# Second mixture: hand-written order in the first three quads, a plain last product, block sums placed anew

## The chip, the cores and the metric

The kernel runs on one core of one Trainium2 chip. The metric is the device time of one execution in microseconds. The core has TensorE (PE in the profile, its weight loads PEld), VectorE (DVE), ScalarE (ACT), GpSimd (POOL) and SyncE (SP), whose queue issues nearly all DMAs here.

## The reference

Attention with a feature map gives x (2304 rows of 512). A first mixture sends each row to one of 8 experts. The part that the change touches is the second mixture: every row goes through all 8 experts, weighted by a matrix P that is normalized eight times by rows and columns.

```python
def _moe2_ref(x, w_gate, w1, w2):          # N, D, E, F = 2304, 512, 8, 1024
    logits = x @ w_gate
    P = np.exp(logits - logits.max())
    for _ in range(8):
        P /= P.sum(1, keepdims=True) + 1e-09
        P /= P.sum(0, keepdims=True) + 1e-09
        P *= N / E
    out = np.zeros((N, D), dtype=np.float32)
    for e in range(E):
        h = np.maximum(x @ w1[e], 0.0)
        out += P[:, e:e + 1] * (h @ w2[e])
    return out
```

## The kernel before

The second mixture is `moe2`. Every float32 operand is split into a rounded high part (ACT, the `..._high` functions) and the rest (DVE, `..._low`), and a product takes three matmuls: high by high, high by low, low by high.

The rows are worked on in three passes of 768 rows (two halves of 3 tiles of 128). A pass runs over 16 weight sets (8 experts, two quarters of the hidden width each). One pass over one weight set is a quad; there are 48 (`NQD`), 16 in a pass (`NW`), and the second pass takes the sets in reverse, so that set 0 is used by quads 31 and 32 in a row. The first product of a quad (x by w1) is done by a scheme of seven block products instead of eight (`mm`, banks `pa`, `pb`, `pd`): numbers 1, 6, 7, 2, 5, 3, 4 in this order, each of six matmuls of 384 columns for each of two halves g of the hidden block. A quad (n) has two groups (n, 0) and (n, 1).

In the first pass the second product is plain: a `piece` is one tile of 128 rows by 512 columns in 12 matmuls. `group` writes out the order of one group: products, copies, splits, and three places `fill[0..2]` for the three pieces of the quad before. `high[k]` and `low[k]` are the splits that ride along: of w2 in group (n, 0), of the next w1 in group (n, 1). Sums of weight blocks (`sums_w2`, `sums_w1`, on POOL) feed further splits, which are stored to HBM (`wd1`, `wd2`) for the later passes: `sums_low` issues two stores right after its split, `store_w2` three, `store_w1` one of 512 KB for each of four operands.

Quads 0 to 2 (`AUTO`) are left to the compiler's scheduler, which orders them freely. They also hold work that occurs once: the rows of the other two passes are loaded, transposed, multiplied by the gate weights and stored (`other_logits`), and P is normalized (`sinkhorn_start`, `sinkhorn_step`). From quad 3 on everything stands in `manual_schedule`: each queue, SP's too, follows the order of the program. After quad 2 the sums of quads 0 and 1 are scaled by P and P is stored (lines 1319 to 1321).

In passes two and three both products use the seven-block scheme. `first` issues the products of the first layer, `h_of` applies the rectifier and P, POOL combines the hidden blocks (tile `R`), `high` and `low` split them into `H` (groups A to D). `unit` is one product of the second layer, six matmuls into a bank of its own (14 per quad, for the quad before), and `flush` adds it to one of seven block accumulators M1 to M7 in `Z`, on DVE, or by a copy on ACT and a sum on POOL for the five k in `GFL`. At the end of a pass the seven blocks are combined and the four result blocks are transposed and written out (`out_tile`, or `turn_part` and `send` for the last pass). The order is written as a list of times in slots, `at(time, function)`, sorted at the end; 14 slots are a quad, and the times only give the order.

## Time and profile before

| | us |
|---|---|
| median of 3 runs | 1955.12 (1946.89 to 1956.08) |
| profiled execution | 1944.32 |
| its span, first to last instruction | 1942.6 |
| first pass, groups (0,0) to (3,0) | 137.16 (429.40 to 566.56) |
| a steady group of the first pass | 15.6 |
| turn from pass two to pass three | about 1458 to 1478 |
| end, from the last first-layer product | 1908.4 to 1942.6 |

A group is taken from the start of its first copy of bank `pa` (`s<-pa`, line 1126) to that of the next group. In a timeline row stand the start in us from the span's start, the time in us, the engine, the line, the operation, the tiles written and read and the count; in brackets the engine's idle time before it and what ended it. PEclk is the granted share of TensorE's clock.

### The profile page before, as it was taken

The page shows a single profiled execution, that of the slowest core. Times are in us where ns is not written, and L with a number is a line of the kernel's source. Part 1 is how long each engine was busy: PE and PEld are TensorE (multiplying, and loading weights), DVE is VectorE, ACT ScalarE, POOL GpSimd, SP SyncE. Part 2 cuts the span into 40 slices and gives each one's busy share as a digit, 9 for nine tenths or more (in the row PEclk, how much of TensorE's full clock was granted, in tenths as well). Part 3 has the DMA queues.
Part 4 walks back from the last instruction along what each step waited for, and adds up shares of the span by engine and source line. Part 5 has one row for each costly group of instructions (what it writes and reads, how often), then busy time and mean ns, then how long its engine had stood idle before and what let it go on. Part 6 is the DMA issues. An engine that isn't in the chain of part 4 may idle for free.

```text
span 1942.6 us, 34972 instructions
## 1 busy us (share of the span) xinstructions
PE 1892.5 (97%) x13028; PEld 1781.2 (92%) x13028; DVE 1347.6 (69%) x2309; ACT 931.5 (48%) x1679; POOL 747.1 (38%) x652
## 2 busy tenths in 40 slices
PE   9999899989999999999999999999999999999997
PEld 8998799966789988888899999999999999999997
DVE  5777777764876776767757667667786676676665
ACT  5776555545544544444444444444444444444442
POOL 2011442211424343434125445444663444444445
PEclk9999999999999999999999999999999999999999
DMA  7324696648757777777476776777756767767663
GB/s 187 100 65 113 163 332 219 212 145 266 261 201 246 260 244 263 253 256 275 161 241 218 231 238 219 237 240 248 238 170 227 240 219 235 233 219 250 224 202 109
DMA packets 232532, 420.67 MB, mean 217 GB/s; under 512 B 31567, under 2 KB 149215, under 8 KB 232349
## 3 DMA queue, kind: packets, MB, share of 16 engines
q1 hardware_dynamic: 228732, 410.93, 64.5%
q0 software_dynamic: 3456, 7.30, 1.0%
q8 instruction: 106, 1.74, 0.4%
q14 instruction: 78, 0.63, 0.1%
q10 hardware_dynamic: 160, 0.07, 0.0%
HBM read 311.18 MB, written 109.50 MB: 217 GB/s over the span
## 4 chain that ended last, share of the span: by engine, by line
PE 68%; DVE 3%; POOL 1%; DMA 1%; issue 1%; ACT 1%; SPq 0%; POOLq 0%; DVEq 0%; ACTq 0%
PE pu L1357 23%; PE pb L1118 14%; PE py L1153 12%; PE pd L1118 9%; PE pa L1118 9%; POOL acc L1447 1%; POOL hr L1447 0%; DVE hh L1404 0%; DMA acc<-in_moe_w_dram 0%; DVE hh L1139 0%; DVE wc L882 0%; DVE xcl L1016 0%; DMA w<-wd 0%; DVE acc L1372 0%; DVE hr L1396 0%
## 5 line engine op out<-in xcount | busy, mean ns | idle before, releaser
L1357 PE MATMUL pu<-hh,w 128*128 128x384 f32 x2688 | 540.4, 336 | 8.0 <-DVE acc L1447 4.2
L1357 PEld LDWEIGHTS pu<-hh,w 128*128 128x128 f32 x2688 | 473.4, 188 | 9.5 <-DVE acc L1447 4.6
L1447 POOL TENSOR_TENSOR hr<-hr 128x384 f32<-128x384 f32 (+1 forms) x192 | 282.3, 1470 | 289.2 <-DVE hr L1396 166.5
L1118 PE MATMUL pb<-xch,wc 128*128 128x384 f32 x1152 | 297.8, 339 | 1.7 <-ACT v L1126 0.6
L1400 ACT ACTIVATE hh<-hr 128x384 fp32r<-128x384 f32 (+2 forms) x256 | 189.3, 761 | 207.5 <-POOL hr L1447 155.2
L1153 PE MATMUL py<-w,hh 128*128 128x512 f32 x1152 | 287.5, 396 | 0.0
L1404 DVE TENSOR_TENSOR hh<-hr,hh 128x384 fp32r<-128x384 f32 (+2 forms) x256 | 223.1, 881 | 62.8 <-ACT hh L1400 61.5
L1153 PEld LDWEIGHTS py<-w,hh 128*128 128x128 f32 x1152 | 215.4, 189 | 43.1 <-issue 1.9
L1370 POOL TENSOR_TENSOR acc<-acc,s 128x384 f32<-128x384 f32 x147 | 161.9, 1102 | 223.9 <-ACT s L1369 223.8
L1372 DVE TENSOR_TENSOR acc<-pu,acc 128x384 f32<-128x384 f32 x267 | 147.3, 553 | 103.9 <-PE pu L1357 103.0
L1118 PEld LDWEIGHTS pb<-xch,wc 128*128 128x128 f32 x1152 | 210.1, 188 | 9.6 <-ACT v L1126 1.5
L1118 PE MATMUL pa<-xch,wc 128*128 128x384 f32 x768 | 198.8, 338 | 0.1
L1118 PE MATMUL pd<-xch,wc 128*128 128x384 f32 x768 | 197.4, 338 | 0.3 <-DVE c L1211 0.2
L1369 ACT ACTIVATE s<-pu 128x384 f32<-128x384 f32 x147 | 72.1, 491 | 162.0 <-PE pu L1357 161.9
L1118 PE MATMUL pb<-xcl,wc 128*128 128x384 f32 x576 | 148.8, 339 | 0.0
L1118 PEld LDWEIGHTS pa<-xch,wc 128*128 128x128 f32 x768 | 139.8, 187 | 4.0 <-ACT acc L1100 0.6
L1118 PEld LDWEIGHTS pd<-xch,wc 128*128 128x128 f32 x768 | 139.5, 187 | 1.2 <-DVE c L1211 0.9
L882 DVE TENSOR_TENSOR wc<-r,wc 128x512 fp32r<-128x512 f32 x170 | 130.6, 769 | 4.1 <-ACT wc L879 3.7
L879 ACT ACTIVATE wc<-r 128x512 fp32r<-128x512 f32 x170 | 105.8, 623 | 10.6 <-PE pa L1118 9.0
L1118 PEld LDWEIGHTS pb<-xcl,wc 128*128 128x128 f32 x576 | 105.0, 188 | 0.0
L1118 PE MATMUL pa<-xcl,wc 128*128 128x384 f32 x384 | 99.1, 338 | 0.0
L1118 PE MATMUL pd<-xcl,wc 128*128 128x384 f32 x384 | 98.8, 338 | 0.0
(270 smaller groups left out, 2990.2 us busy)
## 6 DMA issues: line engine op xcount, KB each, us to landing
w<-wd SPq DMA_DIRECT2D x224, 512.0 KB
wc<-wd SPq DMA_DIRECT2D x120, 512.0 KB
r<-in_moe_w_dram SPq DMA_DIRECT2D x108, 512.0 KB
wd<-wc SPq DMA_DIRECT2D x64, 512.0 KB
wd<-acc SPq DMA_DIRECT2D x128, 256.0 KB
wd<-w SPq DMA_DIRECT2D x96, 256.0 KB
r<-in_moe_w_dram SPq DMA_DIRECT2D x90, 256.0 KB
acc<-in_moe_w_dram SPq DMA_DIRECT2D x64, 256.0 KB
```

The costliest lines, as they stand in the source:

```text
L879: nc.scalar.activation(wc[i][:, 0], wsrc[i], AF.Copy)
L882: nc.vector.tensor_tensor(wc[i][:, 1], wsrc[i], f32(wc[i][:, 0]), ALU.subtract)
L1118: nc.tensor.matmul(dst, wc[i][:, w, kb, sl], xcb[i][x][:, kb], start=(start and m == 0), stop=(stop and m == 5), skip_group_check=True,)
L1153: nc.tensor.matmul(py, ht[:, i * P : i * P + P], w[:, wt], start=(m == 0), stop=(m == 11))
L1357: nc.tensor.matmul(pu, w[:, wl, kb, g2 * P : g2 * P + P], H[:, hx[kb][xl].start + o], start=(m == 0), stop=(m == 5))
L1369: nc.scalar.activation(tmp, pu, AF.Copy)
L1370: nc.gpsimd.tensor_tensor(t, t, tmp, ALU.add)
L1372: nc.vector.tensor_tensor(t, pu, t, ALU.add)
L1400: nc.scalar.activation(H[:, hx[g][0]], R[:, u:v], AF.Copy)
L1404: nc.vector.tensor_tensor(H[:, hx[g][1]], R[:, u:v], f32(H[:, hx[g][0]]), ALU.subtract)
L1447: eng.tensor_tensor(out_, a, b, op)
```

## The change

All 16 quads of the first pass now stand in the hand-written order. The work that occurs once is cut into small steps and put by `CHORES` behind named places of the groups of quads 0 to 2: `l0` to `l6` are the `low` places, `f0` to `f2` the `fill` places. `T(o, i)` transposes tile i of half-pass o, `L` multiplies it by the gate weights, `Q` turns the result; the row and column steps of the normalization are `rw` and `cl`. The stores of a quad's split weights are issued one group or one quad later than before. Set 0 of `wd1` is not stored any more; its operands are computed again for quads 31 and 32, and in two quads ahead of that `GFL` isn't used. At the turn the output tiles come 1.5 slots later. In the last quad the hidden blocks aren't combined; the second product is eight plain block products (`last_unit`) that add up in eight banks, with one more stored operand (`wd2[8]`), and the seven accumulators are combined on POOL ahead of them.

```diff
--- before.py
+++ after.py
-            r, dh, fh = {1: (a11, 0, 0), 2: (a12, 1, 0), 4: (a22, 1, 1)}[i]
+            r, dh, fh = {1: (a11, 0, 0), 2: (a12, 1, 0), 4: (a22, 1, 1), 7: (a21, 0, 1)}[i]
...
+        def gate_tile(o):
+            return acc0(4 + o % 2)[0:E, 0:TW]
+        def logits(o, src):
-            gt = big.tile([E, TW], F32, name="gt", tag="v")
-            nc.scalar.activation(gt, pg, AF.Copy)
+            nc.scalar.activation(gate_tile(o), pg, AF.Copy)
+        def turn_logits(o):
...
+        others = {}
+        def load_other(k):
+            if k < 12:
+                o, i = divmod(k, TB)
+                others[k] = load_x(tiles(1 + o // 2, o % 2)[i], Z[:, 3072 + D * (k % 2) : 3072 + D * (k % 2) + D])
+        def turn_other(o, i):
+            if i == 0:
...
+            k = TB * (o - 2) + i
+            sl = slice(i * P, i * P + P)
+            transposed(
+                others[k], lambda pt: [(x[:, :, sl], pt[:, 2 * b : 2 * b + 2]) for b, x in enumerate(others["x", o])]
+            )
+            load_other(k + 2)
+            if i == TB - 1:
+                dst = xtd[o // 2 - 1][o % 2].rearrange("(b p) t -> p b t", p=P)
+                for b, x in enumerate(others["x", o]):
+                    nc.sync.dma_start(dst[:, 2 * b : 2 * b + 2], x)
+        def other_logits(o):
+            logits(o, lambda kb: others["x", o][kb // 2][:, kb % 2])
...
-        def sinkhorn_start():
+        sk = {}
...
+        def sinkhorn_columns():
+            v = nc.vector
             pc = ps.tile([P, E], F32, name="pc", tag="T", bufs=2)
-            nc.tensor.matmul(pc, c["ones_f"], cs, start=True, stop=True)
+            nc.tensor.matmul(pc, c["ones_f"], sk["cs"], start=True, stop=True)
             cr = big.tile([P, 1, E], F32, name="cr", tag="cr")
             v.tensor_scalar(cr, pc.unsqueeze(1), 1e-9, None, ALU.add)
             v.reciprocal(cr, cr)
             v.tensor_scalar(cr, cr, float(NTOK // E), None, ALU.mult)
             v.tensor_tensor(lg, lg, cr.to_broadcast([P, NT, E]), ALU.mult)
+        def scale_accs(h):
+            for t in tiles(0, h):
+                nc.scalar.activation(accs[t], accs[t], AF.Copy, scale=lg[:, t, 0:1])
+        def turn_gates():
+            lt = sk["lt"] = Z[:, 5120 : 5120 + E * NT].rearrange("p (e t) -> p e t", e=E)
+            nc.vector.tensor_copy(lt, lg.rearrange("p t e -> p e t"))
...
+            if m == NW - 1:
+                nc.sync.dma_start(wd2[8][0][:, :, g], f32(t[:, :, QF:D]))
...
-        for i in (6, 7, 5, 3):
-            store_w1(0, i)
+        for k in range(2):
+            load_other(k)
...
+        T = lambda o, i: lambda: turn_other(o, i)
+        L = lambda o: lambda: other_logits(o)
+        Q = lambda o: lambda: turn_logits(o)
+        rw, cl = sinkhorn_rows, sinkhorn_columns
+        CHORES = {
+            (0, 0): [("l0", Q(0)), ("l1", Q(1), T(2, 0)), ("l3", T(2, 1)), ("f0", T(2, 2)), ("f1", L(2)),
+                     ("l5", T(3, 0)), ("l6", Q(2)), ("f2", T(3, 1), T(3, 2))],
+            (0, 1): [("l0", L(3)), ("l1", T(4, 0)), ("l2", Q(3)), ("l3", T(4, 1)), ("f0", T(4, 2)), ("f1", L(4)),
+                     ("l5", T(5, 0)), ("l6", Q(4)), ("f2", T(5, 1), T(5, 2))],
+            (1, 0): [("l0", L(5)), ("l2", Q(5)), ("l3", sinkhorn_a), ("f0", sinkhorn_b), ("f1", sinkhorn_c), ("f2", rw)],
+            (1, 1): [("l1", cl, rw), ("f0", cl, rw), ("f1", cl, rw), ("f2", cl, rw)],
+            (2, 0): [("f0", cl, rw), ("f1", cl, rw), ("f2", cl, rw)],
+            (2, 1): [("f0", cl), ("f1", lambda: scale_accs(0), turn_gates), ("f2", lambda: scale_accs(1), store_gates)],
...
-                if n == 0:
-                    fill = [lambda i=i: other_logits(*others[2 * g + i]) if i < 2 else None for i in range(3)]
-                else:
-                    fill = [lambda i=i: piece(n - 1, g, i) for i in range(TB)]
+                fill = [lambda i=i: piece(n - 1, g, i) for i in range(TB)] if n else [none] * 3
...
-                    low[3] = both(low[3], lambda: store_w2(n, 0))
+                    if n == NW - 1:
+                        low[3] = both(low[3], lambda: store_w2(n, 0))
+                    if n:
+                        low[2] = both(low[2], lambda: store_w2(n - 1, 0))
+                        for k, i in zip((0, 1, 3, 4), (6, 7, 5, 3)):
+                            low[k] = both(low[k], lambda i=i: store_w1(n, i))
                     low[6] = both(low[6], lambda: sums_w2(n))
...
-                        def lo(i=i):
-                            w1_low(i, n + 1)
-                            if i in (6, 7, 5, 3):
-                                store_w1(n + 1, i)
-                        low[k] = lo
+                        low[k] = lambda i=i: w1_low(i, n + 1)
...
-                if g:
+                if g and n == NW - 1:
                     low[0] = both(low[0], lambda: store_w2(n, 1))
+                if g and n:
+                    low[1] = both(low[1], lambda: store_w2(n - 1, 1))
                 lead = [lambda: x_logits(0), lambda: x_logits(1)] if n == 0 and g == 0 else ()
+                for place, *fs in CHORES.get((n, g), ()):
+                    lst = fill if place[0] == "f" else low
+                    k = int(place[1])
+                    lst[k] = both(lst[k], *fs)
...
-                if n == 0 and g:
-                    sinkhorn_start()
-                if 1 <= n <= 2:
-                    sinkhorn_step()
-                    sinkhorn_step()
-        for n in range(AUTO):
-            quad(n)
-        for t in accs:
-            nc.scalar.activation(accs[t], accs[t], AF.Copy, scale=lg[:, t, 0:1])
-        store_gates()
...
+        part = lambda hx, o: {g: [slice(r.start + o, r.start + o + 1) for r in hx[g]] for g in range(2)}
+        raws.update({"E": (part(HC, 0), 1, 2), "F": (part(HD, 1), 4, 5)})
...
+            if NW + i == NQD - 1:
+                op = (1, 8, 2, 4)[j]
+                nc.sync.dma_start(f32(op_tile(s)), wd2[op][0 if op == 8 else key(wid[NW + i])])
+            else:
+                nc.sync.dma_start(f32(op_tile(s)), wd2[SORD[j]][key(wid[NW + i])])
...
-            elif k in GFL:
+            elif k in GFL and key(wid[min(NW + i + 2, NQD - 1)]):
...
-            for n in range(AUTO, NW):
+            for n in range(NW):
...
+                    if n == NQD - 1:
+                        at(t + 6.52, c21, g)
+                        at(t + 7.0, lambda n=n: h_of(n, 0, 4, st["c"]))
+                        e = 8.05 if g == 0 else 6.45
+                        at(t + e, high, "E", g)
+                        at(t + e + 0.35, low, "E", g)
+                        e = 12.05 if g == 0 else 7.1
+                        at(t + e, high, "F", g)
+                        at(t + e + 0.35, low, "F", g)
+                        continue
...
+                    if key(m) == 0:
+                        at(B0 - 7, load_raw, m, 7)
+                        g = nc.gpsimd
+                        at(B0 + 4.6, tt, g, s1, a21, a22)
+                        at(B0 + 4.7, tt, g, s2, s1, a11, ALU.subtract)
+                        at(B0 + 4.8, tt, g, a21, a11, a21, ALU.subtract)
+                        at(B0 + 10.4, tt, g, a12, a12, s2, ALU.subtract)
+                        for op, e in ((6, 7.6), (7, 8.6), (5, 10.6), (3, 12.6)):
+                            at(B0 + e, w1_high, op)
+                            at(B0 + e + 0.5, w1_low, op)
...
-                at(B0 + 12.3 + k, out_tile, 1, 1 - k // TB, k % TB)
+                at(B0 + 13.8 + k, out_tile, 1, 1 - k // TB, k % TB)
...
-            i = NQD - NW - 1
-            for s in range(14):
-                at(B0 + s + 0.5, unit, i, s)
-            for s in range(8):
-                at(B0 + s + 1.02, flush, i, s)
-            at(B0 + 2.1, tt, G, M2, M2, M1)
-            at(B0 + 2.2, tt, G, M6, M6, M1)
-            at(B0 + 6.1, tt, G, M3, M3, M5)
-            at(B0 + 6.2, tt, G, M3, M3, M6)
-            at(B0 + 8.1, tt, V, M7, M7, M6)
-            at(B0 + 8.2, tt, V, M5, M5, M7)
-            at(B0 + 8.3, tt, G, M4, M4, M7)
-            for g2 in range(2):
...
+            for e, X, Y in (
+                (6.2, M3, M5), (10.2, M6, M1), (12.1, M2, M1), (12.2, M7, M6), (12.3, M3, M6), (12.4, M5, M7), (14.1, M4, M7)
+            ):
+                at(B0 - 14 + e, tt, G, X, X, Y)
             fin = {}
+            banks = [("C12", 0, "pb"), ("C11", 1, "pb"), ("C12", 1, "Y"), ("C21", 0, "Y"), ("C22", 0, "T"),
+                     ("C21", 1, "T"), ("C22", 1, "pd"), ("C11", 0, "pa")]
+            nb = {"pa": 1, "pb": 2, "pd": 1, "Y": 2, "T": 2}
+            def fin_banks():
+                for nm, g2, tag in banks:
+                    fin[nm, g2] = ps.tile([P, TW], F32, name="pf", tag=tag, bufs=nb[tag])
+            def last_unit(nm, j, B, g2, start):
+                w = op_tile(7 * (NQD - NW - 1) + j)
+                m = 0
+                for wl, xl in ((0, 0), (0, 1), (1, 0)):
+                    for kb in range(2):
+                        hx = {"B11": HA, "B22": HB, "B12": raws["E"][0], "B21": raws["F"][0]}[B]
+                        nc.tensor.matmul(
+                            fin[nm, g2], w[:, wl, kb, g2 * P : g2 * P + P], H[:, hx[kb][xl].start],
+                            start=(start and m == 0), stop=(not start and m == 5), skip_group_check=True,
+                        )
+                        m += 1
+            def last_sum(X, nm, g2):
+                tt(V, X[:, g2], fin[nm, g2], X[:, g2])
...
+            at(B0 + 0.45, fin_banks)
+            u = 0
+            for nm, j, B, start, X in (
+                ("C11", 0, "B11", True, None), ("C21", 1, "B11", True, None), ("C12", 2, "B22", True, None),
+                ("C22", 3, "B22", True, None), ("C12", 0, "B12", False, M3), ("C22", 1, "B12", False, M5),
+                ("C11", 2, "B21", False, M2), ("C21", 3, "B21", False, M4),
+            ):
+                for g2 in range(2):
+                    at(B0 + 0.5 + u, last_unit, nm, j, B, g2, start)
+                    if X is not None:
+                        at(B0 + 1.1 + u, last_sum, X, nm, g2)
+                    u += 1
+            for dh in range(2):
+                for g2 in range(2):
+                    for k in range(TB):
+                        at(B0 + 13.7, turn_part, 1, k, dh, g2)
+            for k in range(TB):
+                at(B0 + 13.8, send, 1, k)
+            for dh in range(2):
+                for g2 in range(2):
+                    for k in range(TB):
+                        at(B0 + 17, turn_part, 0, k, dh, g2)
+            for k in range(TB):
+                at(B0 + 18, send, 0, k)
```

## Rows read from the trace of the kernel before

**Rows 1.** The page: busy time by engine, and the clock in 40 slices

```profile
PE 1892.5 (97%) x13028; PEld 1781.2 (92%) x13028; DVE 1347.6 (69%) x2309; ACT 931.5 (48%) x1679; POOL 747.1 (38%) x652
...
PEclk9999999999999999999999999999999999999999
```

**Rows 2.** Timeline of TensorE at the end: start us, us, engine line op

```profile
1908.38 7.47 PE L1357 MATMUL pu<-hh,w 128*128 128x384 f32 x42
1918.39 6.54 PE L1357 MATMUL pu<-hh,w 128*128 128x384 f32 x36 [2.54 <-DVE acc L1372]
1929.18 4.21 PE L1357 MATMUL pu<-hh,w 128*128 128x384 f32 x12 [4.25 <-DVE acc L1447]
1933.18 3.58 PE L1556 MATMUL pt<-ident,acc 128*128 128x128 f32 x24
```

**Rows 3.** Windows: us, then busy time of each engine; PEclk, DMA share, GB/s

```profile
429.40:566.56 137.16, 127.40 (x610) 97.79 (x609) 97.27 (x204) 69.89 (x135) 43.09 (x43) 0.98 0.69 231
...
544.39:566.56 22.17, 19.56 (x84) 16.36 (x83) 15.37 (x28) 10.29 (x19) 7.49 (x7) 0.85 0.44 147
707.91:723.54 15.63, 15.63 (x80) 14.14 (x79) 10.67 (x16) 6.63 (x13) 7.50 (x7) 1.00 0.67 220
723.54:739.14 15.60, 15.60 (x80) 14.10 (x79) 11.78 (x20) 8.19 (x16) 4.38 (x7) 1.00 0.80 288
```

**Rows 4.** Timeline of all engines at the turn to the third pass

```profile
1461.57 0.41 PE L1431 MATMUL pt<-ident,acc 128*128 128x128 f32 x2 [2.20 <-DVE acc L1447]
1462.22 0.54 DVE L1413 TENSOR_TENSOR z<-pd,z 128x384 f32<-128x384 f32 x1
...
1462.35 0.44 PE L1431 MATMUL pt<-ident,acc 128*128 128x128 f32 x2 [0.37 <-DVE acc L1447]
...
1476.73 1.32 PE L1357 MATMUL pu<-hh,w 128*128 128x384 f32 x6 [0.90 <-ACT xq L1433]
```

**Rows 5.** Timeline of POOL at the end

```profile
1921.58 6.96 POOL L1447 TENSOR_TENSOR acc<-acc 128x768 f32<-128x768 f32 x3
```

**Rows 6.** Windows of the end, as in group 3

```profile
1918.00:1932.00 14.00, 9.36 (x45) 9.04 (x46) 8.24 (x15) 0.00 (x0) 10.38 (x6) 0.86 0.01 1
1932.00:1943.00 11.00, 4.77 (x29) 4.43 (x27) 2.00 (x4) 2.28 (x4) 0.00 (x0) 0.81 0.38 143
```

**Rows 7.** Timeline of all engines in the first quad

```profile
429.27 2.75 PE L949 MATMUL pg<-xq,wg 128*8 128x384 f32 x8
...
440.65 1.11 SPq L934 DMA_DIRECT2D acc<-x2d  x2
...
441.66 0.68 DVE L1104 TENSOR_TENSOR acc<-acc 128x512 fp32r<-128x512 f32 x1
...
442.42 1.19 SPq L1106 DMA_DIRECT2D wd<-acc  x2
...
443.52 0.63 PE L941 MATMUL pt<-ident,acc 128*128 128x128 f32 x4 [0.17 <-DMA acc<-x2d]
```

**Rows 8.** Timeline of ACT at the end

```profile
1938.78 0.60 ACT L1560 ACTIVATE xq<-pt 128x512 f32<-128x512 f32 x1 [1.59 <-DVE xq L1561]
```

**Rows 9.** Timeline of DVE: one step of the normalization in the third quad

```profile
543.79 0.16 DVE L1048 TENSOR_SCALAR cr<-pc 128x8 f32<-128x8 f32 x1
...
545.32 0.27 DVE L1041 RECIPROCAL rs<-rs 128x18 f32<-128x18 f32 x1
...
546.86 0.43 DVE L1044 TENSOR_REDUCE cs<-lg 128x8 f32<-128x144 f32 x1
```

**Rows 10.** One line of the kernel: durations in ns, min/median/max

```profile
L1042 DVE TENSOR_TENSOR lg<-lg,rs x8: 287/301/1043, 497.6 to 546.0; 128x144 f32<-128x144 f32 x8
```

**Rows 11.** Timeline of all engines in a steady quad

```profile
708.39 1.18 SPq L857 DMA_DIRECT2D r<-in_moe_w_dram  x2
...
727.65 0.62 ACT L1100 ACTIVATE acc<-acc 128x512 fp32r<-128x512 f32 x1
...
730.60 0.49 ACT L1126 ACTIVATE z<-pb 128x384 f32<-128x384 f32 x1 [1.80 <-PE pb L1118]
```

More of the change, by code (lines that the diff above doesn't have):

```diff
@@ L943, in transposed @@
                 copy(d, s)
-        def logits(ps_, h, src):
+        def gate_tile(o):
+            return acc0(4 + o % 2)[0:E, 0:TW]
+        def logits(o, src):
             pg = ps.tile([E, TW], F32, name="pg", tag="T", bufs=2)
@@ L949, in logits @@
                 nc.tensor.matmul(pg, wg[:, kb], src(kb), start=(kb == 0), stop=(kb == NKB - 1))
-            gt = big.tile([E, TW], F32, name="gt", tag="v")
-            nc.scalar.activation(gt, pg, AF.Copy)
+            nc.scalar.activation(gate_tile(o), pg, AF.Copy)
+        def turn_logits(o):
             pl = ps.tile([P, TB, E], F32, name="pl", tag="T", bufs=2)
             for i in range(TB):
-                nc.tensor.transpose(pl[:, i], gt[:, i * P : i * P + P], c["ident"][0:E, 0:E])
-            t = tiles(ps_, h)[0]
+                nc.tensor.transpose(pl[:, i], gate_tile(o)[:, i * P : i * P + P], c["ident"][0:E, 0:E])
+            t = tiles(o // 2, o % 2)[0]
             nc.vector.tensor_copy(lg[:, t : t + TB], pl)
-        def other_logits(ps_, h):
-            for i, t in enumerate(tiles(ps_, h)):
-                xr = Z[:, 3072 + D * (i % 2) : 3072 + D * (i % 2) + D]
-                transposed(load_x(t, xr), lambda pt: [(xt[:, :, i * P : i * P + P], pt)])
-            nc.sync.dma_start(xtd[ps_ - 1][h].rearrange("(b p) t -> p b t", p=P), xt)
-            logits(ps_, h, lambda kb: xt[:, kb])
+        others = {}
[5 more added lines that the diff above has]
+            if i == 0:
+                others["x", o] = (
+                    [big.tile([P, 2, TW], F32, name=nm, tag=nm) for nm in ("t2", "t3")] if o % 2
+                    else [xt[:, 2 * b : 2 * b + 2] for b in range(2)]
+                )
[11 more added lines that the diff above has]
+            logits(o, lambda kb: others["x", o][kb // 2][:, kb % 2])
         def load_xt(ps_):
@@ L990, in x_logits @@
         def x_logits(h):
-            logits(0, h, lambda kb: xq[h, kb // 2][:, kb % 2])
+            logits(h, lambda kb: xq[h, kb // 2][:, kb % 2])
         xs = {}
@@ L1238, in moe2 @@
             x_low(i)
-        others = [(ps_, h) for ps_ in range(1, NPASS) for h in range(2)]
         load_w2(0, 0)
         load_w2(0, 1)
-        for i in (6, 7, 5, 3):
-            store_w1(0, i)
+        for k in range(2):
+            load_other(k)
         def both(*fs):
@@ L1487, in moe2 @@
                     at(t + e + 0.5, low, "D", g)
-                for j in range(7):
+                for j in range(7 if n + 1 < NQD else 4):
                     s = 7 * i + j
@@ L1499, in moe2 @@
                     m = wid[n + 1]
-                    for op, e in ((6, 7.7), (7, 8.7), (5, 10.7), (3, 12.7)):
+                    if key(m) == 0:
[8 more added lines that the diff above has]
+                            at(B0 + e + 0.5, w1_low, op)
+                    for op, e in ((6, 7.7), (7, 8.7), (5, 10.7), (3, 12.7)) if key(m) else ():
                         at(B0 + e, lambda op=op, m=m: nc.sync.dma_start(f32(wc[op]), wd1[op][key(m)]))
@@ L1504, in moe2 @@
                         at(B0 + e + 0.5, w1_low, op)
-                        at(B0 + e + 1.1, load_raw, m + 1, op)
+                        at(B0 + e + (6.1 if key(m) == 0 and op == 2 else 1.1), load_raw, m + 1, op)
                 if turn:
@@ L1592, in tile_kernel @@
     wd1 = {i: dram.tile([16, P, 2, 2, 256], F32, name=f"wd1{i}") for i in (6, 7, 5, 3)}
-    wd2 = {i: dram.tile([16, P, 2, 2, 256], F32, name=f"wd2{i}") for i in range(1, 8)}
+    wd2 = {i: dram.tile([16 if i < 8 else 1, P, 2, 2, 256], F32, name=f"wd2{i}") for i in range(1, 9)}
     ptd = dram.tile([E * NT, P], F32, name="ptd")
```

54 lines of the change are left out of this document (22 added, 32 removed).

## The prediction

> **What bounds the kernel now.** I read the page's engine rows first: TensorE is busy for 97% of the span, and its clock is granted nearly in full in every slice [rows 1]. So the question is only where it is not fed. Busy time cannot say it, since matmuls overlap; the spacing of their starts can. Forty-two products of 384 columns take 7.47 us [rows 2], (7.47 - 0.34) / 41 = 0.174 us from start to start, so one "unit" of six costs 1.04 us. The windows by stage come next: in the steady first pass a group (half a quad: seven units and three pieces) lasts 15.6 us, with DVE at 10.7 and 11.8 us of it [rows 3]. That stage has no hole. The stretch of the first three quads has: 137.2 us for seven groups [rows 3]. Last I read the timeline of the end, where the stops of TensorE are printed with their releasers [rows 2], and the turn from the second to the third pass [rows 4].
>
> **Change 1, the end.** In before, after the last first-layer product TensorE runs 42, then 36, then 12 products, with idle of 2.54 and 4.25 us ahead of the last two bursts, both ended by DVE's block sums [rows 2]. Those sums wait in turn for POOL, which does three 768-wide sums in 6.96 us, 2.32 each [rows 5]. After the second stop the clock is granted at 0.81 to 0.86 on average [rows 6], which is a share of time at 1.2 instead of 2.4 GHz: 12 products then take 4.21 us, not 2.2, and 24 transposes 3.58 [rows 2]. The change removes what the stops wait for. The last quad needs no combinations of the hidden blocks (only two more blocks are rounded and split), and its second product is 8 plain products times two halves, 16 units, in 8 banks, against 14 units before: plus 2 x 1.04 us. Nothing is flushed between. The seven block sums go to POOL while the units of the quad before are flushed: 7 x 2.32 = 16.2 us, the last four from about 1906 us, when the three placed earlier are done (estimate: they stand two slots of about 1 us ahead of the last first-layer product); that is some 10 us more with a flush between, to 1917 (estimate), and the last block (M4) is wanted by the last unit but one, at about 1925. The chain of TensorE from 1908.4: 17 units (one left over from the quad before) x 1.04 = 17.7 us, then 24 transposes at 0.11 (four take 0.63, their starts 0.11 apart [rows 7]) = 2.6, then 0.3 for the last sum, of which six transposes of other blocks hide the rest: 1929.0. Of the six output tiles three are now sent during the last units, so the last three find a free buffer. In before the last copy began at 1938.78, behind a buffer that an output DMA still held, and from its end the span took 1942.6 - 1939.38 = 3.2 us [rows 8]. After: two copies of 0.6 on ACT, then 3.2: 1933.5. **Gain 9 us**, between 8 (a little wait for M4 or a weight) and 9.5.
>
> **Change 2, the turn.** Before, the transposes of the output tile stop TensorE for 2.20 and 0.37 us, waiting for DVE's sums, and a unit waits 0.90 for ACT to free a bank [rows 4]. Moving the six output tiles 1.5 slots (3 us) later takes the first transposes behind two units and one product. But that product adds into the bank that DVE's sum at 1462.22 reads first [rows 4], and that sum stands behind the same block sums on DVE, which the change leaves in place. So TensorE, which reaches that product at about 1460.3, stops there for some 2.5 us instead. I count **1 us** of gain, from the bank wait mostly; 0 to 3.5 are the ends (all stops stay, all go).
>
> **Change 3, one weight set not stored.** The first of the 16 weight sets is no longer written at the start and is computed again at the end of pass two: three POOL sums, four more splits on ACT and DVE, and in two quads five flushes on DVE in place of ACT and POOL. DVE is busy for 69% of the span [rows 1], so this fits; for the densest slots I take **0.5 us** lost (0 to 2).
>
> **Change 4, the first three quads by hand.** The work of TensorE is unchanged. From 429.4 us it is: five groups with pieces x 15.6 = 78.0 [rows 3]; two without, 42 x 0.174 each = 14.6; six logits of eight products, 2.65 each (2.75 with the last one's latency [rows 7]) = 15.9; twelve x-tiles of four transposes, 48 x 0.11 = 5.3; small matmuls of gate and normalization, some 3 (estimate). Sum 116.8, so 20.4 us of the 137.2 are lost in before. The hand-written order keeps every queue in the order of the program, SP's too, and that decides what comes back:
> - The x-tiles of the other passes are loaded through two buffers; a tile's load is issued when the tile two before it has been transposed. From issue to the transpose it takes 443.52 - 440.65 = 2.87 us [rows 7]. For T(2,2) the issue stands on SP behind two stores that wait for DVE's split of the weight sums; in before that split runs at 441.66 and the stores are issued until 443.61 [rows 7]. So the load lands at 446.5, while TensorE has only 10.2 us of work from 429.4 (two logits 5.3, three units 3.1, turns and tiles 1.8): 6.9 us lost, since product 5 is queued behind the tile.
> - T(3,2): after product 4 DVE does three steps (1.9 us), SP two stores (1.2), then the load 2.87; TensorE has 1.1 of work meanwhile: 4.8 lost. T(4,2): 2.87 less 1.7 = 1.1. T(5,2): 2.87 less 0.7 = 2.2.
> - The normalization: one step of rows and columns costs DVE about 2.5 us (543.79 to 545.59 without a break, then 0.30 and 0.43 [rows 9, 10]). Group (1,1) gets four: 11.8 - 2.1 (pieces of quad 0 are copied by ACT) + 10 = 19.7 us against 16.4 of TensorE; group (2,0) three: 10.7 + 7.5 = 18.2 against 16.2. Excess 5.3, of which 3 is lag that a piece and two products cover at the next group: 2.2 lost.
> - The stop of before at the gate's store, with the clock lost in it (0.85 over 22.17 us [rows 3], so 3.3 us of work), is gone: scaling and turning lie behind pieces.
>
> Sum lost after: 6.9 + 4.8 + 1.1 + 2.2 + 2.2 = 17.2, plus 1 for a clock that may fall in one of the longer stops. **Gain 20.4 - 18.2 = 2 us**; ends -4 and +15 (below).
>
> **Change 5, stores moved in quads 1 to 15.** Four 512 KB stores per quad go from its second group to the next quad's first. Steady groups carry 220 and 288 GB/s [rows 3]; I take 0, covered by 2 to 3 us between ACT's split of the sums and the next copy that TensorE waits for [rows 11].
>
> **Sum**: 9 + 1 - 0.5 + 2 = 11.5 us. The profiled execution took 1944.3 us (1.7 around its span): 1932.8. The median shown is 1955.1, 10.8 above it, and nothing in the change touches that spread, so I forecast 1955.1 - 11.5 = **1943.5** for the median.
>
> **Rivals.**
> 1. The loads are hidden (DVE gets to the weight sums earlier, so SP's stores don't hold the tile loads). Then of 17.2 us some 5 to 7 stay, change 4 gives 12 and the time is 1933.5. For it: SP has little else to do then. Against: the order of SP is fixed by the program.
> 2. Each of the two long stops also costs the clock, as the stop in the window from 544.39 did, 3.3 us each [rows 3]: change 4 is -4, the time 1949.5. For it: two stops of 5 to 7 us are longer than the 4.25 us after which it fell at the end [rows 2, 6]. Against: the 0.98 of the whole stretch is used up by that one window, so the many shorter stops did not lower it.
> 3. POOL's sums lengthen the normalization: a product of two operands on DVE took 0.30 us at the median and 1.04 at most [rows 10]. Seven steps have 14 such operations in groups where POOL works; if all met it, 14 x 0.74 = 10.4 us are added and the total gain is 1: 1954. The Trainium skill, "SBUF — State Buffer", section "SBUF: two separate sides", says that a DVE operation with two SBUF inputs and a GpSimd operation exclude each other for the whole instruction; by that rule this would be the case wherever the two meet. In the trace only a few of the operations show it.
> 4. Slower than before: the stores of change 5 back up. Before ACT's next split of the sums, from the issue at 708.39 to 727.65 in the steady quad [rows 11], the queue would have to move 5,376 KB (weights 1,536, stores 3,840), 5.5 MB in 19.3 us; TensorE feels it after another 2.3 us, when the copy at 730.60 is late, so from below 255 GB/s. At 240 it is 1.3 us in each of 14 quads, 18 us: 1962. It outweighs the gain from 245 GB/s down. Against it: at 288 GB/s the engines are busy 0.80 of the time [rows 3].
>
> **How the numbers follow.** Forecast 0.47 (1938 to 1949 by its bounds), rival 1 0.20, rival 2 0.20, rival 3 0.05, rival 4 0.08. The range 1928 to 1956 holds the first three cases and most of the fourth. About 0.5% (9.8 us) is what a measurement tells from no change. Faster by more: two thirds of the forecast, all of rival 1, little of rival 2: 0.55. Slower by more: rival 4, 0.08. The rest, 0.37.
>
> **What would show it.** End: the stops of 2.54 and 4.25 us gone, 17 units without a break, clock 1.0, last output copy about 9 us earlier. Turn: a stop at the product ahead of the first output tile. Early quads: stops of TensorE at the transposes of the third tile of each set, released by a DMA from x2d; DVE near full in two groups. Wrong would make me: no stop at these tiles, block sums of POOL later than the last units, or ACT waiting for the stores of the weight sums in every quad.

## The result, and the profile after

The changed kernel takes 1966.5 us (median of 8 runs) against 1955.6 for the kernel before (8 runs): a ratio of 1.0061, 95% interval 1.0045 to 1.0077. It is slower by some 11 us, where 11.5 us of gain were forecast. The profiled execution of the changed kernel has a span of 1964.7 us. Two lines of its page answer to [rows 1]:

```profile
PE 1902.5 (97%) x13040; PEld 1791.7 (91%) x13040; DVE 1358.9 (69%) x2313; ACT 927.9 (47%) x1683; POOL 735.5 (37%) x640
...
PEclk9998999997999999999999999999999999999999
```

The clock row dips in the tenth slice (0.7), which is 442 to 491 us: the first quad. Windows over the groups of that stretch (us, then busy time of PE, PEld, DVE, ACT, POOL with their instructions, PEclk, DMA share, GB/s) answer to [rows 3]; a group begins where ACT copies its first product:

```profile
439.50:478.70 39.20, 26.58 (x101) 17.08 (x101) 20.70 (x27) 15.67 (x33) 12.97 (x11) 0.77 0.33 98
478.70:500.60 21.90, 18.27 (x89) 12.16 (x89) 10.23 (x18) 12.64 (x30) 4.00 (x4) 0.94 0.53 175
500.60:520.30 19.70, 19.70 (x94) 15.12 (x93) 10.40 (x18) 9.00 (x18) 7.43 (x8) 1.00 0.92 320
520.30:541.20 20.90, 18.50 (x95) 16.01 (x94) 18.33 (x48) 9.47 (x19) 3.88 (x5) 1.00 0.34 114
541.20:562.90 21.70, 18.32 (x79) 16.19 (x78) 19.21 (x47) 6.58 (x14) 8.39 (x9) 0.84 0.74 261
...
439.50:594.70 155.20, 133.17 (x611) 105.04 (x611) 103.06 (x201) 71.85 (x148) 47.02 (x45) 0.91 0.56 188
```

The last line is the whole stretch of seven groups, the part of the kernel that change 4 reorders: 155.2 us, where before had 137.2 [rows 3] and 135 were forecast. The first group alone takes 39.2 us. The fourth and fifth have DVE at 18.3 and 19.2 us. From the eighth group on they take 15.6 to 15.8 us as in before, but for one pair (16.9 and 14.7; before 17.2 and 14.7).

The timeline of the first two groups and the normalization shows the stops (start, us, engine, line, operation; in brackets the idle time before and what ended it):

```profile
443.65 1.99 POOL L871 TENSOR_TENSOR s<-r 128x512 f32<-128x512 f32 x1
...
446.38 2.02 DVE L1032 TENSOR_TENSOR t<-t,xq 128x768 f32<-128x768 f32 x1
...
448.32 2.02 DVE L1039 TENSOR_TENSOR xcl<-t,xch 128x768 fp32r<-128x768 f32 x1
...
450.40 0.99 PE L1158 MATMUL pb<-xcl,wc 128*128 128x384 f32 x2 [3.62 <-DVE xcl L1039]
...
460.89 1.08 PE L940 MATMUL pt<-ident,acc 128*128 128x128 f32 x4 [2.84 <-DMA acc<-x2d]
...
475.69 1.08 PE L940 MATMUL pt<-ident,acc 128*128 128x128 f32 x4 [4.31 <-DMA acc<-x2d]
...
533.25 0.36 PE L1078 MATMUL pc<-cs,ones_f 128*128 128x8 f32 x2 [2.03 <-DVE cs L1073]
...
553.44 0.57 PE L1078 MATMUL pc<-cs,ones_f 128*128 128x8 f32 x2 [3.29 <-DVE cs L1073]
```

The two stops that a DMA ends are the third tiles T(2,2) and T(3,2) of the prediction. The one before them, 3.62 us at the third block's first product, is in no term of it: DVE's differences of 768 columns take 2.02 us there while POOL works. The last two are the normalization.

The end went as forecast. Of the stops in [rows 2] nothing is left, and the last transposes begin 2.2 us after the last twelve products do:

```profile
1955.92 2.33 PE L1621 MATMUL pf<-hh,w 128*128 128x384 f32 x12
...
1958.10 1.47 PE L1635 MATMUL pt<-ident,acc 128*128 128x128 f32 x12
...
1959.39 1.08 ACT L1641 ACTIVATE xq<-pt 128x512 f32<-128x512 f32 x2 [2.31 <-PE pt L1635]
```

From the start of the last first-layer matmul to the end of the span it is 25.8 us in the changed kernel, 34.4 in the first profile of before.

### The profile page after: what moved, and what is told of

It reads as the page before. It is cut to its first block, busy times and chain, and to the rows that moved or that the text cites. A ratio compares the mean times of both kernels' runs of the same rounds, so it can differ in the third digit from the quotient of the medians.

```text
span 1964.7 us, 35037 instructions
## 1 busy us (share of the span) xinstructions
PE 1902.5 (97%) x13040; PEld 1791.7 (91%) x13040; DVE 1358.9 (69%) x2313; ACT 927.9 (47%) x1683; POOL 735.5 (37%) x640
## 4 chain that ended last, share of the span: by engine, by line
PE 69%; DVE 6%; issue 1%; DMA 1%; POOL 1%; ACT 1%; SPq 0%; ACTq 0%; DVEq 0%; POOLq 0%
PE pu L1408 21%; PE pb L1158 14%; PE py L1193 13%; PE pd L1158 9%; PE pa L1158 9%; DVE hh L1455 1%; PE pf L1621 1%; DVE xcl L1039 1%; DVE acc L1423 1%; PE pg L951 1%; DVE wc L881 1%; DMA acc<-x2d 0%; POOL hr L1498 0%; DVE hr L1447 0%; DMA w<-wd 0%
## 5 line engine op out<-in xcount | busy, mean ns | idle before, releaser
L1408 PE MATMUL pu<-hh,w 128*128 128x384 f32 x2604 | 523.7, 335 | 1.2 <-DMA w<-wd 1.2
L1408 PEld LDWEIGHTS pu<-hh,w 128*128 128x128 f32 x2604 | 458.2, 188 | 1.5 <-DMA w<-wd 1.5
L1498 POOL TENSOR_TENSOR hr<-hr 128x768 f32<-128x768 f32 x186 | 274.4, 1475 | 293.6 <-DVE hr L1447 203.1
L1193 PE MATMUL py<-w,hh 128*128 128x512 f32 x1152 | 282.8, 394 | 0.0
L1421 POOL TENSOR_TENSOR acc<-acc,s 128x384 f32<-128x384 f32 x135 | 147.9, 1096 | 219.9 <-ACT s L1420 219.9
L1420 ACT ACTIVATE s<-pu 128x384 f32<-128x384 f32 x135 | 66.4, 492 | 157.8 <-PE pu L1408 157.8
```

The costliest lines, as they stand in the source:

```text
L1193: nc.tensor.matmul(py, ht[:, i * P : i * P + P], w[:, wt], start=(m == 0), stop=(m == 11))
L1408: nc.tensor.matmul(pu, w[:, wl, kb, g2 * P : g2 * P + P], H[:, hx[kb][xl].start + o], start=(m == 0), stop=(m == 5))
L1420: nc.scalar.activation(tmp, pu, AF.Copy)
L1421: nc.gpsimd.tensor_tensor(t, t, tmp, ALU.add)
L1498: eng.tensor_tensor(out_, a, b, op)
```

## The experiments

Eleven more kernels ran, and before once more. Two numbers are read from each: the ratio of its time to before's on the same chip, with the 95% interval (before's median lay at 1955.0, 1952.6 and 1945.1 us beside the three sets of runs, so times in us of different sets are not compared; the changed kernel was measured beside a set of its own, so a difference from its ratio is good to some 4 us), and the length of the **stretch** of seven groups, from ACT's copy of the first group's first product to that of the eighth group. The stretch is read from one profile each; the two of before differ by 2.1 us in it.

| kernel | ratio to before | stretch, us |
|---|---|---|
| before, two profiles | 1 | 137.2, 139.2 |
| changed | 1.0061 (1.0045 to 1.0077) | 155.2 |
| e1_end | 0.9964 (0.9948 to 0.9980) | 137.6 |
| e2_auto | 0.9952 (0.9933 to 0.9971) | 131.8 |
| e3_pool | 1.0078 (1.0058 to 1.0097) | 154.9 |
| e4_noload | 1.0008 (0.9994 to 1.0021) | 147.6 |
| e5_early | 1.0042 (1.0028 to 1.0057) | 151.3 |
| e6_both | 1.0000 (0.9986 to 1.0013) | 140.4 |
| e7_keep | 0.9941 (0.9924 to 0.9959) | 132.2 |
| e8_half | 1.0026 (1.0015 to 1.0038) | 148.9 |
| e10_place | 0.9983 (0.9973 to 0.9993) | 137.2 |
| e11_spread | 1.0004 (0.9988 to 1.0019) | 141.5 |
| e12_keep2 | 1.0003 (0.9992 to 1.0015) | 140.4 |

**Is the later start part of it?** (e0_again) The profiles of before and of the changed kernel differ by 22.1 us, and 10.1 of these are there before the second mixture begins.

> The kernel before, unchanged, profiled a second time. Between the two profiles the changed kernel starts its second mixture 10.1 us later (first group's copy at 439.5 against 429.4 us), on instructions that are the same up to there. If that is a spread between executions, in which the first profile of before (1944.3 us, its median is 1955.6) was a low one, this profile gives about 1955 us and the copy near 439 us. If the change causes it, the copy stands at 429.4 again.

It took 1956.0 us. The first logits of the second mixture, at 429.27 in the first profile of before [rows 7], stand here at 439.74:

```profile
439.74 2.75 PE L949 MATMUL pg<-xq,wg 128*8 128x384 f32 x8
```

In the changed kernel they stand at 439.56. So these 10 us are a spread of the unchanged kernel, not the change. In the three sets of runs the profiles begin the first group at 440 to 443, 433 to 438 and 427 to 430 us, so the start goes with the set more than with the kernel; what sets it stays open. Against this second profile of before the account of the spans closes: start -0.4, stretch +16.0, the rest of the first pass -0.5, second and third pass +2.7, end -7.2; sum 10.6, measured 10.5.

**The end alone** (e1_end). The edit is the diff's end block, `load_op`, the raws E and F and the eighth store, in the kernel before.

> The kernel before with the new end alone: the last quad's second product plain in eight banks, its block sums placed ahead, output transposes during the last units. Theory A (the end gives what was forecast, the early quads lose it): 9 us below before, 1946.5. Rival (the end's gain is lost in the whole, the stops move into the units before): within 2 us of before, 1953 to 1956.

It came to 0.9964, 7 us less (4 to 10). From the last first-layer matmul to the end it takes 25.7 us against 34.4 and 33.0 in the two profiles of before: the gain of 7 to 9 us is real, as theory A said. In this profile some 3 us of it are lost where the second pass begins (change 5, below).

**The hand-written order against the scheduler's** (e2_auto), with the same instructions:

```diff
+        AUTO = 3
...
+        for n in range(AUTO):
+            quad(n)
...
         with tc.manual_schedule():
-            for n in range(NW):
+            for n in range(AUTO, NW):
```

> The changed kernel, with its first three quads left to the scheduler again; the same instructions, chores, end, turn and moved stores. Theory A (the hand-written order of the three quads costs the time): some 18 us below the changed kernel, 1948, and the stretch from the first group's copy to that of the fourth quad back at about 137 us. Rival B (the moved stores, the recomputed weight set or the later start cost it): 1960 or more.

It came to 0.9952, some 21 us below the changed kernel, and the stretch to 131.8 us, less than before's own. Its window over the stretch:

```profile
441.60:573.40 131.80, 124.30 (x611) 96.56 (x611) 100.57 (x203) 71.62 (x147) 43.51 (x44) 1.00 0.69 228
```

Beside the changed kernel's line above, the same 611 matmuls keep TensorE busy for 133.17 instead of 124.30 us, at a clock of 0.91 instead of 1.00: 8.9 us go with the clock. The other 14.5 of the 23.4 us are idle time (22.0 against 7.5). The hand order is the cause, and the moved stores are not, since this run has them too; which of its places, the next runs ask.

**POOL beside DVE, first try** (e3_pool):

```diff
-                    if more:
+                    if more and n:
                         sums_w1(n + 1)
...
+                    if n == 0:
+                        low[3] = both(lambda: sums_w1(1), low[3])
```

> The changed kernel with one thing moved in its first group: POOL's three sums for the second weight set are issued after DVE's third low product instead of at the group's head, so that they don't run beside DVE's differences of 768 columns, which took 2.02 instead of 0.94 us there. Theory C (this contention makes the stop of 3.8 us at the first product of the third block, and with it the clock falls): the stop goes, the group's granted clock rises above 0.77, 5 to 8 us gained, 1959 to 1961. Rival D (the tile loads hold the group anyway, the time saved is waited at the third tile): within 2 us of the changed kernel, 1964.5 to 1968.

It came to 1.0078 with the stretch at 154.9: no gain. But the run didn't test theory C. POOL runs its own queue, nothing made the three sums wait, and they ran from 446.6 us on, beside the same differences, which took 2.02 us again. A later place in the program is no later time where no dependency holds it.

**The tile loads** (e4_noload):

```diff
-            if k < 12:
+            if 2 <= k < 12:
+                others[k] = others[k - 2]
+            elif k < 12:
```

> The changed kernel without ten of the twelve loads of x tiles of the other passes: the transposes read the first two tiles again, so the output is not the reference's. What is left out: ten 256 KB loads and the waits for them. Theory D (the loads through two buffers hold the first two groups): the four stops at third tiles, 3.16 + 4.47 + 1.82 + 1.09 = 10.5 us in the changed kernel, are gone, and the time is 10 to 12 us lower, 1955. Rival E (TensorE would wait there for DVE, ACT and the transposes' banks anyway): under 5 us, 1961.5 or more.

By the ratio it is 10 us below the changed kernel, which is what theory D forecast for all four stops. The trace shows less: the stretch lost 7.6 us, as much as the two stops at T(2,2) and T(3,2) (3.16 and 4.47 us from start to start beyond a transpose). Those at T(4,2) and T(5,2) stayed, so the forecast of the time came out in part by luck. TensorE's rows of this run say what they are:

```profile
446.33 1.01 PE L1160 MATMUL pb<-xcl,wc 128*128 128x384 f32 x2 [3.56 <-DVE xcl L1041]
452.88 1.97 PE L940 MATMUL pt<-ident,acc 128*128 128x128 f32 x8 [0.81 <-ACT acc L936]
464.29 1.32 PE L940 MATMUL pt<-ident,acc 128*128 128x128 f32 x8 [1.04 <-ACT t L936]
475.68 0.66 PE L940 MATMUL pt<-ident,acc 128*128 128x128 f32 x4 [1.66 <-DVE lg L959]
484.14 0.66 PE L940 MATMUL pt<-ident,acc 128*128 128x128 f32 x4 [1.04 <-ACT t L936]
485.72 0.69 PE L940 MATMUL pt<-ident,acc 128*128 128x128 f32 x2 [0.93 <-ACT t L936]
```

The transposes, the logits, the turned gates and the small products of the normalization share two banks (`tag="T", bufs=2`). Where two tiles stand together, the next waits until ACT or DVE has emptied one. Theory D holds for two of its four stops.

**POOL beside DVE, second try** (e5_early): the same three sums, issued before the first quad.

> The changed kernel with POOL's three sums for the second weight set issued before the first quad, where the scheduler put them in the kernel before, so that they can't run beside DVE's 768-column differences in the first group (in the run where they were moved behind DVE in the program, POOL ran them at the same moment all the same, since nothing held it). Theory C (contention of POOL and DVE makes the first stop of 3.8 us and brings the clock down): the differences take 0.95 instead of 2.02 us, the stop falls below 1 us, and 4 to 8 us are gained, 1959 to 1962. Rival D (the saved time is waited at the third tile): 1964 to 1968.

It came to 1.0042, 3.9 us off the stretch. The differences take 0.94 us and the first stop is gone; but T(2,2) waits longer:

```profile
442.77 0.94 DVE L1032 TENSOR_TENSOR t<-t,xq 128x768 f32<-128x768 f32 x1
443.64 0.94 DVE L1039 TENSOR_TENSOR xcl<-t,xch 128x768 fp32r<-128x768 f32 x1
...
455.29 1.09 PE L940 MATMUL pt<-ident,acc 128*128 128x128 f32 x4 [4.29 <-DMA acc<-x2d]
```

So the contention made the stop (theory C), and 1.3 us of what was saved are waited at the tile, from start to start (a part of D). The clock did not come back: it falls behind the stop at T(2,2) instead (0.50 from 451 to 460 us).

**Both** (e6_both).

> Both of the last two: ten loads of x tiles left out (the output is not the reference's), and POOL's sums ahead of the first quad. If the two causes add and are the whole, the first two groups lose no clock either: 10.5 + 3.8 of stops and some 6 of clock, 1946, the time of the run with the scheduler's order. If each is hidden behind the other, it gives more than the sum of the two alone. If something else holds the groups (the transposes' banks, the normalization), 1952 or more.

The stretch fell by 14.8 us, where the two alone give 7.6 + 3.9 = 11.5. In the first group alone, 39.1 us in the changed kernel (39.3 in e8_half, where its code is the same), the two save 8.0 and 2.4 us alone and 13.6 together. Its window tells why:

```profile
436.00:461.50 25.50, 22.17 (x101) 13.84 (x101) 17.02 (x26) 15.66 (x33) 6.80 (x8) 0.93 0.27 88
```

Its clock is 0.93; it is 0.77 in the changed kernel, 0.78 without the loads alone, and 0.77 with POOL's sums early alone. The same 101 matmuls are busy for 22.17 instead of 26.58 us. As long as one of the two causes is left, the clock stays down. The times do not show more than the sum: by the ratios the three runs are 10, 4 and 12 us below the changed kernel. And 140.4 us is still 8.6 more than the scheduler's order: the causes named were not the whole, as the last case of the expectation has it.

**The normalization** (e8_half): the second and fourth of the fourth group's four steps and the first and third of the fifth group's three are left out.

> The changed kernel with four of the eight normalization steps left out, two of four in the fourth group and two of three in the fifth (so the gates are not fully normalized). Theory G (DVE is the bound of these two groups, and the clock falls behind its stops): the stops of 0.53, 2.19 and 3.45 us go and with them the clock of 0.84 in the fifth group, 3.5 us of 21.7: 6 to 9 us less than the changed kernel, 1957.5 to 1960.5. Rival (pieces cover the normalization): within 2 us, 1964.5 or more.

The stretch lost 6.3 us, and by the ratio the time 7. Of the normalization's three stops none is left (one of 1.53 us behind DVE's other work comes in their place), and the fifth group runs at full clock in 17.6 instead of 21.7 us:

```profile
526.60:544.20 17.60, 16.07 (x82) 14.28 (x82) 12.44 (x23) 6.87 (x14) 7.95 (x7) 1.00 0.91 312
```

Theory G holds. Added up, the named causes nearly reach the scheduler's order: taking 14.8 and 6.3 from 155.2 leaves 134.1, 2.3 us above it. No run has all three at once.

**Another order by hand** (e10_place), with all of the computation:

```diff
+        sums_w1(1)
...
-            (0, 0): [("l0", Q(0)), ("l1", Q(1), T(2, 0)), ("l3", T(2, 1)), ("f0", T(2, 2)), ("f1", L(2)),
-                     ("l5", T(3, 0)), ("l6", Q(2)), ("f2", T(3, 1), T(3, 2))],
+            (0, 0): [("l0", Q(0), T(2, 2)), ("l1", Q(1), T(3, 0)), ("f0", T(3, 1)), ("f1", L(2), T(3, 2)),
+                     ("f2", Q(2), T(4, 0))],
...
-                lead = [lambda: x_logits(0), lambda: x_logits(1)] if n == 0 and g == 0 else ()
+                lead = [both(lambda: x_logits(0), T(2, 0)), both(lambda: x_logits(1), T(2, 1))] if n == 0 and g == 0 else ()
```

and the second group likewise, one tile behind each product.

> The changed kernel with the whole computation and another hand-written order of its first two groups: the twelve x tiles stand one behind each product, two of them between the logits at the head, so that two products or a set of logits lie between a tile's load and its transposes, and POOL's sums for the second weight set stand ahead of the first quad. Theory H (it is the places in the order, not that it is fixed, that cost the time): the stops of 3.2, 4.5 and 3.8 us go, with the clock, as in the run with both left out (14.8 us), and some of the waits between tiles placed together: 14 to 20 us, 1946 to 1952. Rival (the tiles' waits for banks, copies or buffers come in their place): 1958 or more.

The stretch came to 137.2 us, 18.0 less, and the time to 0.9983, 15 us below the changed kernel and just below before. Theory H holds: most of the loss isn't that the order is written by hand, but where it puts the tiles and POOL's sums. One stop behind a tile's load is left, of 2.19 us. Its window over the stretch,

```profile
429.80:567.00 137.20, 127.33 (x611) 100.10 (x611) 101.57 (x202) 71.04 (x148) 41.71 (x43) 0.96 0.64 214
```

has TensorE busy 3.0 us longer than in the scheduler's order, at a clock of 0.96, and idle 2.4 us longer: the 5.4 us that are left.

> The last one, with the normalization moved as well: two, three and two or three steps in three groups instead of four, three and one in the same, and the scaling of the sums and the gates' store one group later. By theory G the 6 to 9 us of the fourth and fifth group come back, less one to three us that DVE still holds: 3 to 8 us below the run before it. Rival (the steps wait as long wherever they stand, 6.8 us of stops in the scheduler's order too): within 2 us of it.

This (e11_spread) fell: the stretch grew by 4.3 us. TensorE waits 7.9 us in four stops for the normalization, 5.9 in four in the run before it, and the gates' store, now in the seventh group ahead of its pieces, stops it behind DVE's turning of the gates:

```profile
555.75 0.61 PE L1098 MATMUL pq<-ident,acc 128*72 128x128 f32 x2 [3.26 <-DVE acc L1091]
```

> The last one, with the first weight set stored at the start and read back instead of computed again: 2 us below it, by the spacing of the groups at the end of the second pass, as it was with the scheduler's order. If the hand-written order is then as good as the scheduler's it is within 3 us of that run, 0.994 of before; better than 0.993, and the order by hand gives something of its own.

In this run (e12_keep2) the spacing of the groups at the end of the second pass, 2.4 us longer in the run before it, is that of the kernel before again. The times of these two runs can't be told apart, since their intervals overlap nearly whole. And the order by hand is not as good as the scheduler's: that run, with the first weight set stored, is the next one; its stretch is 8.2 us shorter and its ratio lower by 12 us.

**The recomputed weight set** (e7_keep), on the scheduler's order, with `GFL` used in all quads again:

```diff
+        for i in (6, 7, 5, 3):
+            store_w1(0, i)
...
-                    if key(m) == 0:
-                        at(B0 - 7, load_raw, m, 7)
...
```

> The run with the three quads left to the scheduler, and the first weight set stored at the start and read back as in the kernel before, instead of computed again at the end of the second pass. The spacing of the groups there grew by 2.2 us in the changed kernel between the 27th and the 30th of the second and third pass. Theory F (the recomputation costs that): 2 us less than that run, 1944. Rival (the four stores at the start cost as much): 1946.

It came to 0.9941, 11.5 us below before (8 to 15) and the best of all; it beats both kernels. Against e2_auto it is 2 us, which the times alone do not tell from nothing, since the intervals overlap. The spacing of the groups at the end of the second pass is that of before within 0.1 us; in the changed kernel and in the run with the scheduler's order it is 2.2 to 2.4 us longer. The windows of these two quads, first of the changed kernel, then of this one, then of before, show what is short there:

```profile
1411.50:1470.90 59.40, 58.22 (x327) 56.53 (x326) 57.62 (x80) 24.83 (x42) 31.44 (x19) 1.00 0.46 141
```

```profile
1381.90:1439.20 57.30, 57.30 (x329) 57.30 (x328) 49.42 (x66) 27.64 (x48) 36.94 (x25) 1.00 0.56 185
```

```profile
1383.60:1440.60 57.00, 57.00 (x327) 57.00 (x327) 49.47 (x68) 26.66 (x46) 36.40 (x24) 1.00 0.56 187
```

DVE is busy for 57.6 of 59.4 us in the changed kernel, against 49.4 of 57.3 in this run.

## Why the prediction was wrong

**Change 4 is the step that failed**: forecast a gain of 2 us, with ends of 4 lost and 15 gained; measured a loss of 16 to 18. What failed is its list of losses: POOL's sums beside DVE and the waits for the two banks stand in it at nothing, the clock at 1 us, and most of the normalization as covered. By its own account, 155.2 - 116.8 = 38.4 us are lost, not 18.2:

| term | forecast | measured |
|---|---|---|
| T(2,2) and T(3,2), behind their loads | 11.7 | 7.6 |
| T(4,2) and T(5,2) | 3.3 | 2.9, but behind banks, not loads: near by luck |
| other tiles that wait for a bank | 0 | 3.5 (three of 1.1 to 1.2) |
| third block's first product, behind DVE beside POOL | 0 | 3.8 |
| normalization | 2.2 | 6.2 |
| clock, and waits under 0.4 us | 1 | 14.4 (the rest) |

- The tile loads were right in mechanism and place at T(2,2) and T(3,2), so rival 1 did not happen. T(3,2) costs 4.5 us where 4.8 were forecast. T(2,2) costs 3.2, not 6.9, and 4.5 without the stop ahead of it (e5_early). In that run its transposes begin 17.4 us after the group's start, as forecast (446.5 - 429.4 = 17.1); but TensorE reaches the tile after 13.1 us, not 10.2, as it waits 1.33 and 0.81 us at the two tiles ahead.
- POOL's sums were costed in the normalization only (rival 3), where a few operations met them. The place where they met DVE head on is the first group. In the kernel before the scheduler had run the second weight set's sums long before it, from 263 us on; the hand-written order runs them at 443.65. The step looked at the chores in the diff and should have looked at every instruction that the scheduler had moved ahead.
- The normalization: I let three of its 5.3 us of excess be covered by a lag. The run with half of it gives back 6.3.
- The clock is the largest miss. Rival 2 had it at 3.3 us a stop, two stops. In the first group it fell behind the first stop, stayed at 0.50 until behind T(2,2), came back, and fell again behind T(3,2) (windows below). Against the scheduler's order it is 8.9 us in the stretch.
- The base was wrong too: all 20.4 us that before lost were taken as open to recovery, and only named stops as losses of after. The scheduler's order at full clock still loses 131.8 - 116.8 = 15.0, of which 6.7 are the normalization's stops and the rest single waits of under 1 us. No order that was tried got below that.

POOL's timeline of the kernel before, with the first of the three sums:

```profile
263.17 1.29 POOL L872 TENSOR_TENSOR s<-r 128x512 f32<-128x512 f32 x1 [12.48 <-DMA r<-in_moe_w_dram]
```

Windows of the changed kernel's first group (the clock is the third number from the end):

```profile
439.50:446.32 6.82, 6.82 (x24) 2.43 (x24) 6.59 (x6) 3.77 (x6) 6.66 (x6) 1.00 0.01 2
446.32:455.00 8.68, 5.06 (x18) 3.82 (x18) 8.68 (x11) 3.99 (x7) 3.21 (x2) 0.74 0.05 5
455.00:462.00 7.00, 3.35 (x14) 2.57 (x14) 0.87 (x3) 1.32 (x4) 1.44 (x2) 0.50 0.67 221
462.00:469.00 7.00, 7.00 (x28) 4.38 (x28) 2.22 (x4) 3.70 (x9) 0.00 (x0) 0.85 0.48 152
469.00:478.70 9.70, 4.36 (x22) 3.89 (x21) 2.33 (x6) 2.89 (x8) 1.65 (x2) 0.78 0.43 119
```

The same from the end of the first stop to behind T(2,2), from there to the stop at T(3,2), and behind that:

```profile
450.40:463.80 13.40, 9.74 (x34) 7.64 (x34) 5.47 (x10) 4.24 (x10) 1.44 (x2) 0.50 0.43 124
463.80:471.50 7.70, 6.55 (x32) 3.84 (x31) 4.56 (x9) 4.69 (x11) 0.65 (x1) 0.98 0.35 129
...
475.60:480.00 4.40, 4.31 (x15) 4.34 (x16) 0.00 (x0) 1.67 (x4) 0.00 (x0) 0.50 0.49 142
```

**Change 1**: forecast 9, measured 8.6 against the first profile, from which it was worked out, and 7.2 against the second, where the later of the two stops took 2.53 us and not 4.25. The mechanism is right, stop by stop; the lower end of 8 was too high for a part that differs by 1.4 us between two profiles of before.

**Change 2**: forecast 1 us (0 to 3.5), measured 0.1 to 0.2 by the groups' spacing. The stop moved to the product named, with 2.1 us of idle, 2.3 from start to start beyond a product, where 2.5 were named and [rows 4] had 2.20 and 0.37 at the transposes, so next to nothing was gained:

```profile
1493.75 0.61 PE L1158 MATMUL pd<-xch,wc 128*128 128x384 f32 x2 [2.09 <-DVE z L1464]
```

**Change 3**: forecast 0.5 (0 to 2), measured 2.2 to 2.4. DVE's share of the whole span (69%, [rows 1]) was the wrong view; in the two quads themselves it is 97%.

**Change 5**: forecast 0, and the steady groups are unchanged at 15.6 to 15.8 us: rival 4 did not happen. One thing stays open: the passage from the first to the second pass took 0 to 3.2 us longer in the runs with the changed end (0.8 in the changed kernel, 3.0 in e1_end, 0.0 and 3.2 in e8_half and e10_place, which have the same code there). A product of the second layer waits there for its weights from HBM: 0.35 us in before, 1.16 in the changed kernel, 1.83 in e1_end, 0.31 and 1.94 in the last two. The eighth store of the last weight set falls in it, but it was not tried alone.

**The rest of the argument** held: most of the spread of 10.8 us between the profiled execution and the median lies ahead of the second mixture (of the 11.6 us between the two profiles of before 10.5 do), so differences were rightly taken from the traces and set on the median. With the scheduler's order the terms are 8 for the end, 0 for the turn, 2.3 lost to the recomputation and 6 from the stretch, 11.7 in all; that run measured 9 (6 to 13).

## What to carry to other kernels

Where an order written by hand takes the place of a scheduler's, list what the scheduler had run early on the engines that the diff doesn't name, and put it ahead by hand; and space the users of a two-buffer load or a two-bank tag at least one load or one copy apart. A few stops of 3 to 5 us that follow each other cost clock on top (in the first group 11.4 us of long stops, and matmuls that are busy 4.4 us longer than without them), and removing one of them need not bring it back, so cost them as a group and not one by one; and read the cover for added DVE work from the stage's own windows, not from the page's share.

## What the runs showed of the hardware

- DVE's difference of two 768-column operands in SBUF takes 0.94 us alone and 2.02 us beside POOL's sums, and POOL's sums of 512 columns take 1.9 to 2.0 instead of 1.29 us: each takes nearly as long as one of both in turn (0.94 + 1.29 = 2.23). The Trainium skill, "SBUF — State Buffer", section "SBUF: two separate sides", says that such a pair exclude each other for a whole instruction; the trace agrees here, where both engines have one such instruction after another, and the two runs with POOL's sums moved and not moved show what it costs: 3.8 us of stop.
- After a stop of TensorE of 3.6 us the granted clock was 0.50 (1.2 instead of 2.4 GHz) for 13.4 us, with waits of 0.81 and 2.84 us in them; it was 0.98 for the next 7.7 us and 0.50 again behind a stop of 4.3 us. Once the three long stops were gone, it was 0.93 over the whole group.
- One kernel, unchanged, reaches the same instruction at 429.3 us in one execution and at 439.7 in another.
